# A convolution and gated two-layer network on one core: the first step's exchanges, loads and copies put in another order

## The chip, the cores and the metric

The kernel runs on one core of a Trainium2 chip. The metric is the device time of one execution in microseconds (us). A core has five engines that run their own instruction streams: TensorE (PE in the profile; its weight loads are PEld), VectorE (DVE), ScalarE (ACT), GpSimd (POOL) and SyncE (SP). SP, GpSimd and ScalarE also issue transfers (DMA), which sixteen DMA engines carry out. Results of matrix products come to lie in PSUM, eight banks of 128 x 512 words, here named `slot`; everything else is in SBUF, 128 partitions wide.

## The reference: what is computed

A causal depthwise convolution with seven taps, then two matrix products with a gate between them, in float32:

```python
w = exp(weight - max); w = w / (sum(w) + 1e-9)          # 8 heads x 7 taps
y[b, s, :] = sum_k w[head, k] * x_pad[b, s + k, :]      # x: 8 x 4096 x 192, 24 channels per head
h = y.reshape(32768, 192) @ w_in                        # w_in: 192 x 2048
g = h * (1 / (1 + exp(-1.702 * h)))
out = g @ w_out                                         # w_out: 2048 x 192
```

`x` and the taps come as float32; `w_in` and `w_out` come as 64-bit floating point, so the kernel itself takes their words apart and rounds them to 32 bits.

## The kernel before, in words

**Tiling and steps.** The tokens are worked through in 32 steps, which the code numbers by `big`; each has 1024 tokens, 512 consecutive ones of two sequences, the first 256 of each in one half of the partitions and the other 256 in the other half. A step transposes its x to channels on partitions (`transpose_x`, VectorE, L143), convolves it (`conv`, seven multiply-adds on VectorE, L162 and L164) into `own`, multiplies by `w_in` (the first product), applies the gate on ScalarE (`gelu`, L235) into the big buffer `g`, multiplies `g` by `w_out` (the second product, L513), transposes back and stores. From the second step on the first product runs at L212 as three passes: x and the weights are split into a high part, a low part and a difference (`xh`, `xl`, `xd` of x, `wh`, `wl` and stage tiles of the weights). The high parts `wh` and half of the low parts stay in SBUF, while the other parts stream from a scratch in DRAM, `w_dram`, through seven places of `ring` (`load_ring`, L199).

**Step 0** (`first_step`, with `second_plain` for its second product) does the same work while the weights themselves are still being loaded and prepared. `w_in` comes in four parts (`raw`, L321), each with 256 columns in one half of the partitions and the next 256 in the other. Each goes through `take` (exponent and mantissa, VectorE, L371 and L372), `clamp` (two ACTIVATEs on ScalarE, L377 and L378), `join` (L386 and L389) and `rounded` (L397). `split` is `take` and `clamp` together. From a rounded part, `top` makes `wh` (ScalarE, L425), `rest` the remainder (VectorE, L428), `spread` the low part (ScalarE, L435) and `differ` the difference (VectorE, L439). `put` stores a part's pieces to `w_dram` (L449). Then `w_out`, again in four parts (`raw_out`, L326), goes through the same rounding, in the order 1, 2, 3, 0.

Since a half of the partitions holds only half the columns of a part of `w_in`, each half of x must also meet the weights of the other half. So x is exchanged between the halves: `exchange` (L672) issues two SBUF-to-SBUF transfers on SP. `swapped[c]` are the exchanged copies of `own` in the place of `xt`; `swapped_h`, `swapped_l` and `swapped_d` those of `xh`, `xl` and `xd`, in places of `wh` and `wl` that are not in use yet. The first product of step 0 goes in sixteen groups: groups 0 to 3 with the first part of the weights in plain float32 (`plain`, L691), groups 4 to 15 in three passes (`quick`, L682), four groups a part: the first two on the core's own x, the next two on the exchanged x. A group takes up two banks of PSUM, and ScalarE's gelus of a group free them for the group four places on.

Behind the first product, `second_plain` starts (L513), and at its first row the rest of the preparation is issued: part 0's `top`, `rest`, `spread`, `differ` and `put`; `across`, which copies the finished halves of `wh` and `wl` to the other half of the partitions (L443); the split of step 1's x; the first loads of the ring; and the sums of the second product's weights (`FORMS_O`) on VectorE. Step 1's first product (`unit`, L212) follows on PE.

**What sets the order.** The order is written out by hand: each engine, and each engine's DMA queue, carries out its instructions in the order of the program, and an instruction waits for the semaphores of what it needs. So a transfer that waits on SP holds back every later transfer of SP, and a clamp on ScalarE stands behind the gelus that are written ahead of it. In `first_step` SP issues x's first batch, `w_in`'s first part, x's second batch and the other parts; then the exchanges of own for the three channel groups, xh, xl, the first part of `w_out`, and xd. GpSimd issues the stores of part 1 and the three other parts of `w_out`. SP follows with the stores of part 2, the x of step 1, the stores of part 3 and the x of step 2. Two of the three channel groups of step 0's convolution are done on PE with diagonal weights (`first_conv`, L657), the third on VectorE.

Of the kernel before, what the change touches and what calls it, by code (L numbers as in the profile page):

```python
# [16 lines left out]
def kernel(  # L17
# [9 lines left out]
    nc = tc.nc  # L27
# [10 lines left out]
    T = 256  # L38
# [32 lines left out]
    def wide(t):  # L71
        return t.bitcast(F32)
# [52 lines left out]
    def load_x(big, ns=(0, 1), os=(0, 1), queue=nc.sync):  # L125

        p, c = divmod(big, CHUNKS)
        xin = xin_of(big)
        if c == 0 and (ns[0], os[0]) == (0, 0):
            vec.memset(xin[0:R, :, 0, :], 0.0)  # L130
        for n in ns:
            for o in os:
                j = 1 if c == 0 and o == 0 else 0
                t = c * TOK + o * T + (j - 1) * Q
                for v in range(2):
                    q0 = o * R + v * Q
                    queue.dma_start(  # L137
                        out=xin[q0 : q0 + Q, n, j:NJ, :],
                        in_=x_v[n, p, t : t + (NJ - j) * Q, v * Q : v * Q + XW].rearrange("(j i) d -> i j d", i=Q),
                    )  # L140
# [13 lines left out]
    def own_of(c, of=own):  # L154
        return of[:, 2 * c : 2 * c + 2, :]
# [9 lines left out]
                out=dst, in0=src, scalar=tap, in1=dst, op0=ALU.mult, op1=ALU.add  # L165
            )

    def split_high(src=own):
        act.mul(xh, src, NEAR)

    def split_low(src=own):
        vec.scalar_tensor_tensor(out=xl, in0=src, scalar=UP, in1=wide(xh), op0=ALU.mult, op1=ALU.subtract)  # L172
# [146 lines left out]
    def load_w_in(i):  # L319
        for o in range(2):  # L320
            nc.sync.dma_start(  # L321
                out=raw[i][halves[o], :].bitcast(U32).rearrange("p (k f) -> p k f", k=NC), in_=w_in_v[2 * i + o]
            )

    def load_w_out(i, queue=nc.sync):
        queue.dma_start(  # L326
            out=raw_out[i].bitcast(U32).rearrange("p (c d) -> p c d", c=CW),
            in_=w_out_v[:, i * CW : (i + 1) * CW, :],
        )

    load_x(0, (0,))
    load_w_in(0)
    load_x(0, (1,))
    for i in range(1, N_IN):
        load_w_in(i)

# [43 lines left out]
    def split(piece):  # L380
        take(piece)
        clamp(piece)
# [55 lines left out]
        for r in range(2):  # L438
            vec.tensor_sub(stage(i)[:, 2 * r], wide(lows(i)[r]), half(wide(pair_of(i)), r))  # L439

    def across(t):
        for o, queue in enumerate((nc.sync, nc.gpsimd)):
            queue.dma_start(out=wide(t[halves[1 - o], N_IN:]), in_=wide(t[halves[o], :N_IN]))  # L443

    def put(i, queues=(nc.gpsimd, nc.gpsimd)):
        for o, queue in enumerate(queues):
# [251 lines left out]
    def first_step(tiles):  # L698

        for c in (1, 2):  # L700
            for k in range(K):
                act.mul(diag[:, c - 1, k, :], ident, cw[:, c, k : k + 1])
        for c in (1, 2, 0):
            transpose_x(0, c, 0, 1)
        first_conv(1, 0)
        first_conv(2, 0)
        for k in range(K):
            conv(0, k, n=0)
        split(part(0))
        for c in (1, 2, 0):  # L710
            transpose_x(0, c, 1, 2)
        first_conv(1, 1)
        act.copy(own_of(1), pairs[1][0].rearrange("p (n t) -> p n t", n=2))
        first_conv(2, 1)
        join(part(0))
        exchange(swapped[1], own_of(1))
        for k in range(K):
            conv(0, k, n=1)
        exchange(swapped[0], own_of(0))
        act.copy(own_of(2), pairs[1][1].rearrange("p (n t) -> p n t", n=2))  # L720
        exchange(swapped[2], own_of(2))
        rounded_in(0)
        early = osbs[:, 0 : 2 * NC * T].rearrange("p (b t) -> p b t", t=T)
        pieces = (1, 2, 3, 0)
        one, two, three, last = (part(N_IN + i) for i in pieces)
        split_high()
        exchange(wide(swapped_h), wide(xh))
        split(part(1))
        take(part(2))
        clamp(part(2))  # L730
        split_low()
        exchange(wide(swapped_l), wide(xl))
        load_w_out(pieces[0])
        round_w_in(1)

        def products(*groups):
            for i in groups:
                (quick if i >= 4 else plain)(tiles, i // 4, i // 2 % 2, i % 2)

        def gelus(*groups):  # L740
            for i in groups:
                r, s = 4 * (i // 4) + i % 2, i // 2 % 2
                for h in range(2):
                    gelu(tiles[(r + 2 * h) % 4], r + 2 * h, (h ^ s,))

        products(0, 1)
        gelus(0)
        top(1)
        gelus(1)
        split_both()  # L750
        exchange(wide(swapped_d), wide(xd))
        rest(1)
        spread(1)
        split(part(3))
        differ(1)
        put(1)
        for a in pieces[1:]:
            load_w_out(a, nc.gpsimd)
        round_w_in(2)
        products(2, 3)  # L760
        gelus(2, 3)
        top(2)
        products(4)
        gelus(4)
        join(part(3))
        rest(2)
        spread(2)
        rounded_in(3)
        top(3)
        differ(2)  # L770
        put(2, (nc.sync, nc.sync))
        load_x(1)
        products(5, 6)
        gelus(5, 6)
        rest(3)
        take(one)
        products(7)
        spread(3)
        gelus(7)
        clamp(one)  # L780
        differ(3)
        take(two)
        put(3, (nc.sync, nc.sync))
        round_w_out(pieces[0])
        products(8, 9)
        gelus(8, 9)
        clamp(two)
        take(three)
        round_w_out(pieces[1])
        products(10, 11)  # L790
        gelus(10, 11)
        clamp(three)
        products(12, 13)
        gelus(12, 13)
        take(last)
        round_w_out(pieces[2])
        products(14)
        gelus(14)
        clamp(last)
        products(15)  # L800
        gelus(15)
        round_w_out(pieces[3])
        for c in range(NC):
            transpose_x(1, c)
        for k in range(K):
            for c in range(NC):
                conv(c, k, early)

        pf, pa, pb, pc = tiles[3], tiles[1], tiles[0], tiles[2]
        load_x(2)  # L810

        def at(i):
            if i == 0:
                top(0)
                rest(0)
                spread(0)
                differ(0)
                put(0, (nc.sync, nc.gpsimd))
                across(wh)
                across(wl)  # L820
                split_high(early)
                split_low(early)
                split_both(early)
                for i in range(STREAM, STREAM + RING):
                    load_ring(i)
                for c in range(NC):
                    transpose_x(2, c)
                for item in FORMS_O:
                    add_form(*item)

        turns = second_plain(pb, pa, pc, at)
        unit(1, [pf], 0)
        for m, n, src in turns:
            turn(m, n, src, slice(0, TOK // Q))
            if m:
                store(0, n)
        return [pf, pa, pb, pc]
# [57 lines left out]
```

## Time and profile before

| | |
|---|---|
| median of 3 runs | 2179.86 us (2176.53 to 2179.95) |
| profiled execution | 2179.55 us, its span 2177.8 us |
| PE busy | 2165.8 us, 99% of the span |
| DVE, ACT, POOL busy | 1776.9, 986.6, 327.6 us |
| first plain product (L691) starts | 20.50 us |
| first quick product (L682) starts | 30.48 us |
| second product of step 0 (L513) starts | 62.94 us |
| step 1's first product (L212) starts | 104.28 us |

The profile gives, for one execution, the busy time of each engine, groups of instructions by line of the code, the chain of work that ended last (followed back from the end, at each step to what released it), the waits with their releasers, and the transfers with their sizes and their time from issue to landing. A row such as `slot<-xh,wh` names the tile written and the tiles read, without numbers of buffers. Times are counted from the start of the span. Busy time of PE is modelled with overlap, so a busy share of 99% does not say that PE runs at its peak; the granted clock is given beside it, where 1.00 is full. GB/s of the stretches is what the DMA engines moved, and a share somewhat above 1 in a stretch comes from packets that reach over its edges.

### The profile page before, as it was taken

To read this page: it belongs to the slowest core of one execution; us is meant where nothing else is said; L and a number is where in the kernel's file an instruction comes from. 1 tells how busy PE (TensorE), PEld (TensorE's weight loads), DVE (VectorE), ACT (ScalarE), POOL (GpSimd) and SP (SyncE) were. 2 spreads that over 40 slices of the span, in tenths; PEclk is the share of its full clock that TensorE was granted. 3 is DMA by queue.
4 is the path that set the end of the run, shared out by engine and by line. 5 is a ranking of instruction groups with operands and counts; after the bars stand their busy time and mean duration, and the time that the engine had idled before them with its cause. 6 is when DMAs were issued, how large, how long until landed. Compare 5 with 4: busy or idle time off the path is not lost.

```text
span 2177.8 us, 66287 instructions
## 1 busy us (share of the span) xinstructions
PE 2165.8 (99%) x28998; PEld 1521.4 (70%) x28998; DVE 1776.9 (82%) x2500; ACT 986.6 (45%) x2104; POOL 327.6 (15%) x444
## 2 busy tenths in 40 slices
PE   8999999999999999999999999999999999999999
PEld 7477766677766777667777667776677766677766
DVE  7888888888887878888888878788888888787766
ACT  6344444444444544444444445444444444444443
POOL 1101121011111111110111111111101111111000
PEclk9999999999999999999999999999999999999999
DMA  9666666575665666665756657565666666575554
GB/s 268 170 161 165 161 144 146 138 179 147 165 147 130 172 157 161 147 144 143 177 151 157 150 129 179 151 165 145 139 152 172 156 152 150 126 186 147 137 119 99
DMA packets 264707, 336.66 MB, mean 155 GB/s; under 512 B 121169, under 2 KB 226577, under 8 KB 264289
## 3 DMA queue, kind: packets, MB, share of 16 engines
q0 software_dynamic: 42848, 145.37, 31.8%
q1 hardware_dynamic: 219920, 186.66, 30.4%
q8 instruction: 227, 3.72, 0.7%
q10 hardware_dynamic: 1648, 0.39, 0.1%
q14 instruction: 64, 0.52, 0.1%
HBM read 199.43 MB, written 29.88 MB: 105 GB/s over the span
## 4 chain that ended last, share of the span: by engine, by line
PE 97%; DMA 1%; DVE 1%; SPq 0%; issue 0%; DVEq 0%
PE slot L513 50%; PE slot L212 46%; PE slot L682 1%; DMA wl<-xd 1%; DMA ring<-w_dram 0%; DMA g<-in_x_dram 0%; SPq L137 0%; DVE own L164 0%; DVE osbs L500 0%; DVE w_form L389 0%; DVE xl L172 0%; DVE w_form L386 0%; DVE xd L175 0%; DVE w_form L397 0%; SPq L510 0%
## 5 line engine op out<-in xcount | busy, mean ns | idle before, releaser
L513 PE MATMUL slot<-g,w_form 128*32 128x256 f32 x8928 | 894.1, 379 | 0.0
L235 ACT ACTIVATE g<-slot 128x512 f32<-128x512 f32 x1024 | 556.2, 596 | 506.7 <-PE slot L212 501.2
L576 DVE TENSOR_TENSOR g<-g 128x1024 f32<-128x1024 f32 x403 | 483.7, 1219 | 213.2 <-ACT g L235 124.5
L513 PEld LDWEIGHTS slot<-g,w_form 128*32 128x32 f32 x8928 | 480.6, 110 | 138.1
L624 ACT COPY room<-slot 32x256 f32<-32x256 f32 x651 | 238.3, 366 | 627.4 <-PE slot L513 625.3
L513 PE MATMUL slot<-g,w_out_s 128*32 128x256 f32 (+1 forms) x6336 | 508.8, 392 | 0.0
L212 PE MATMUL slot<-xh,wh 64*128 64x512 f32 x2976 | 422.6, 389 | 0.0
L212 PE MATMUL slot<-xd,ring 64*128 64x512 f32 x2976 | 418.6, 387 | 0.2 <-DMA ring<-w_dram 0.2
L513 PEld LDWEIGHTS slot<-g,w_out_s 128*32 128x32 f32 x6336 | 254.0, 110 | 204.1 <-issue 38.7
L164 DVE SCALAR_TENSOR_TENSOR own<-xt,cw,own 128x512 f32<-128x512 f32 (+1 forms) x552 | 365.7, 731 | 0.4
L212 PEld LDWEIGHTS slot<-xh,wh 64*128 64x128 f32 x2976 | 276.7, 184 | 69.8 <-issue 13.2
L212 PEld LDWEIGHTS slot<-xd,ring 64*128 64x128 f32 x2976 | 278.9, 184 | 59.1 <-DMA ring<-w_dram 0.6
L581 POOL DMA_DIRECT2D g<-g x124 | 117.1, 944 | 759.4 <-PE slot L513 520.8
L513 PE MATMUL slot<-osbs,w_form 128*32 128x256 f32 x2232 | 225.3, 379 | 0.0
L137 POOL DMA_DIRECT2D g<-in_x_dram x232 | 155.3, 676 | 401.1 <-PE slot L513 397.4
L212 PE MATMUL slot<-xl,wl 64*128 64x512 f32 x1488 | 209.4, 387 | 0.0
L212 PE MATMUL slot<-xl,ring 64*128 64x512 f32 x1488 | 209.1, 386 | 0.0
L513 PE MATMUL slot<-room,w_form 128*32 128x256 f32 x2232 | 171.6, 379 | 0.0
L212 PEld LDWEIGHTS slot<-xl,wl 64*128 64x128 f32 x1488 | 139.5, 184 | 30.0
L212 PEld LDWEIGHTS slot<-xl,ring 64*128 64x128 f32 x1488 | 139.5, 184 | 29.3
L513 PEld LDWEIGHTS slot<-osbs,w_form 128*32 128x32 f32 x2232 | 117.5, 110 | 42.5
L576 DVE TENSOR_TENSOR room<-slot,room 96x256 f32<-96x256 f32 x248 | 100.1, 414 | 57.1 <-PE slot L513 55.0
(114 smaller groups left out, 1379.0 us busy)
## 6 DMA issues: line engine op xcount, KB each, us to landing
ring<-w_dram SPq DMA_DIRECT2D x744, 192.0 KB, 2.7
g<-g POOLq DMA_DIRECT2D x124, 512.0 KB, 6.6
g<-in_x_dram POOLq DMA_DIRECT2D x220, 180.0 KB, 4.7
out_dram<-osbs SPq DMA_DIRECT2D x186, 128.0 KB, 5.5
g<-osbs POOLq DMA_DIRECT2D x31, 512.0 KB, 5.6
g<-room POOLq DMA_DIRECT2D x31, 512.0 KB, 6.6
g<-in_moe_w_in_dram SPq DMA_DIRECT2D x8, 384.0 KB, 9.5
w_dram<-ring SPq DMA_DIRECT2D x10, 288.0 KB, 5.0
```

Of the source, the lines that this page charges most:

```text
L137: queue.dma_start(out=xin[q0 : q0 + Q, n, j:NJ, :], in_=x_v[n, p, t : t + (NJ - j) * Q, v * Q : v * Q + XW].rearrange("(j i) d -> i j d", ...
L164: vec.scalar_tensor_tensor(out=dst, in0=src, scalar=tap, in1=dst, op0=ALU.mult, op1=ALU.add)
L212: nc.tensor.matmul(slot[o], w(o)[halves[o], k, :], t[halves[o], 2 * k : 2 * k + 2, :], start=first and k == KS[0], stop=last and k == KS[- ...
L235: act.activation(g[:, r // NG, :, o, r % NG, :], slot[o].rearrange("p (n t) -> p n t", n=2), AF.Gelu_apprx_sigmoid,)
L513: nc.tensor.matmul(dst, w, t, start=first, stop=last, skip_group_check=True)
L576: (eng.tensor_add if op == "+" else eng.tensor_sub)(v(dst), v(a), v(b))
L581: nc.gpsimd.dma_start(out=spot(dst), in_=spot(a), accum_op=ALU.add)
L624: act.copy(to, d)
L682: nc.tensor.matmul(tiles[2 * h + r][h ^ s], w[halves[h], c, :], xs[s][halves[h], 2 * c : 2 * c + 2, :], start=n == 0 and c == KS[0], stop= ...
```

## The change

Only step 0 is touched, in five places.

- x's second batch is issued on SP ahead of the first part of `w_in`. On VectorE, the transposes of that batch and four of the seven taps of its convolution move ahead of the first part's `take`; its `join` follows behind the last three taps. On SP the exchange of own's second channel group is issued before the convolution's last taps in program order.
- The exchange of xh is dropped. ScalarE makes `swapped_h` from the exchanged own instead, with a second `split_high`, behind `spread(1)`; `split_high` gets a destination for it.
- The first part of `w_out` (piece 1) is loaded behind the exchange of xd and behind `differ(1)` in program order, no longer ahead of it.
- The stores of part 1 and the other three loads of `w_out` are issued by SP instead of GpSimd; `load_w_out` loses its queue argument.
- `across` takes a range of parts. Parts 1 to 3 are copied behind the last quick product and step 1's convolution, ahead of the load of step 2's x; part 0 in the old place.

```diff
-    def split_high(src=own):
-        act.mul(xh, src, NEAR)
+    def split_high(src=own, dst=xh):
+        act.mul(dst, src, NEAR)
...
-    def load_w_out(i, queue=nc.sync):
-        queue.dma_start(
+    def load_w_out(i):
+        nc.sync.dma_start(
...
     load_x(0, (0,))
+    load_x(0, (1,))
     load_w_in(0)
-    load_x(0, (1,))
...
-    def across(t):
+    def across(t, i0, i1):
         for o, queue in enumerate((nc.sync, nc.gpsimd)):
-            queue.dma_start(out=wide(t[halves[1 - o], N_IN:]), in_=wide(t[halves[o], :N_IN]))
+            queue.dma_start(out=wide(t[halves[1 - o], N_IN + i0 : N_IN + i1]), in_=wide(t[halves[o], i0:i1]))
...
         for k in range(K):
             conv(0, k, n=0)
-        split(part(0))
         for c in (1, 2, 0):
             transpose_x(0, c, 1, 2)
+        for k in range(4):
+            conv(0, k, n=1)
+        split(part(0))
         first_conv(1, 1)
         act.copy(own_of(1), pairs[1][0].rearrange("p (n t) -> p n t", n=2))
         first_conv(2, 1)
+        exchange(swapped[1], own_of(1))
+        for k in range(4, K):
+            conv(0, k, n=1)
         join(part(0))
-        exchange(swapped[1], own_of(1))
-        for k in range(K):
-            conv(0, k, n=1)
         exchange(swapped[0], own_of(0))
...
         split_high()
-        exchange(wide(swapped_h), wide(xh))
         split(part(1))
...
         exchange(wide(swapped_l), wide(xl))
-        load_w_out(pieces[0])
         round_w_in(1)
...
         spread(1)
+        split_high(xt[:, :, :, 0:T].rearrange("p c n t -> p (c n) t"), swapped_h)
         split(part(3))
         differ(1)
-        put(1)
+        load_w_out(pieces[0])
+        put(1, (nc.sync, nc.sync))
         for a in pieces[1:]:
-            load_w_out(a, nc.gpsimd)
+            load_w_out(a)
...
         pf, pa, pb, pc = tiles[3], tiles[1], tiles[0], tiles[2]
+        across(wh, 1, N_IN)
+        across(wl, 1, N_IN)
         load_x(2)
...
                 put(0, (nc.sync, nc.gpsimd))
-                across(wh)
-                across(wl)
+                across(wh, 0, 1)
+                across(wl, 0, 1)
```

## The prediction, as it was put on record

> **What bounds the kernel now.** I read the page's head first, then the chain of waits in order of time, then stretches of the span, then the transfers. The head tells little by itself:
>
> ```profile
> span 2177.8 us, 66287 instructions
> ```
>
> The span stands beside 2179.55 us for the same execution (1.75 us lie around it), and 2179.86 us is the median of the runs shown, 0.31 above; the sum is made against 2179.55. The chain, with start, length and what ended last:
>
> ```profile
> 5.78 7.22 DMA g<-in_x_dram
> ...
> 28.90 12.10 DMA wl<-xd
> ...
> 41.05 21.96 PE slot L682 x164
> 63.01 41.34 PE slot L513 x384
> 104.35 5.66 PE slot L212 x47
> ```
>
> TensorE (PE) sets the end from 41.05 on without a break, so step 0 is worth what the moment is worth at which its second product (L513, 63.01) starts. Ahead of that stand two transfers: x's second batch (till 13.0) and the exchange of xd (till 41.0). The stretches show what the second costs (columns: PE, weight loads, VectorE = DVE, ScalarE = ACT, GpSimd, granted clock, DMA share, GB/s; the counts take in matmuls that overlap an edge):
>
> ```profile
> 36.80:39.00 2.20, 0.00 (x0) 0.00 (x0) 2.20 (x4) 2.20 (x5) 0.00 (x0) 1.00 0.96 311
> 39.00:41.00 2.00, 0.50 (x1) 0.18 (x1) 1.12 (x3) 0.16 (x1) 0.00 (x0) 0.72 1.02 410
> 41.00:43.00 2.00, 1.95 (x10) 1.58 (x12) 0.00 (x0) 0.69 (x2) 0.00 (x0) 0.50 1.01 406
> 43.00:45.00 2.00, 2.00 (x12) 1.59 (x10) 0.56 (x1) 0.81 (x2) 0.00 (x0) 0.50 1.04 417
> 45.00:46.90 1.90, 1.90 (x12) 1.49 (x10) 0.26 (x1) 1.27 (x3) 0.00 (x0) 0.55 1.03 411
> ...
> 50.00:62.90 12.90, 12.90 (x115) 11.53 (x111) 9.60 (x16) 10.79 (x19) 0.00 (x0) 1.00 0.75 195
> sum 32.90, PE 29.14 PEld 25.08 DVE 23.54 ACT 24.97 POOL 5.00; mean PE 3.24 PEld 2.79 DVE 2.62 ACT 2.77 POOL 0.56
> ```
>
> PE stops at 36.80, runs one matmul at 39, and goes on at 41.05: 4.25 us less one matmul, 4.1 lost. Then the clock is granted at 0.50 to 0.55 until 46.9. At full clock a matmul comes every 12.90/115 = 0.112 us (0.113 with the edges); the chain's 164 would take 18.6 us and took 21.96: 3.4 lost. The stall is worth 7.5 us in all. The sum row covers 30.0 to 62.9 and will be needed for ACT.
>
> Next the transfers, each with its KB and its median time from issue to landing:
>
> ```profile
> g<-in_moe_w_in_dram SPq DMA_DIRECT2D x8, 384.0 KB, 9.5
> ...
> w_dram<-ring POOLq DMA_DIRECT2D x4, 288.0 KB, 9.1
> xt<-own SPq DMA_DIRECT2D x6, 128.0 KB, 6.1
> wh<-xh SPq DMA_DIRECT2D x2, 384.0 KB, 7.1
> wh<-xl SPq DMA_DIRECT2D x2, 384.0 KB, 9.3
> g<-in_moe_w_out_dram SPq DMA_DIRECT2D x1, 768.0 KB, 11.6
> wl<-xd SPq DMA_DIRECT2D x2, 384.0 KB, 11.4
> g<-in_moe_w_out_dram POOLq DMA_DIRECT2D x1, 768.0 KB, 11.3
> ...
> g<-in_x_dram SPq DMA_DIRECT2D x4, 180.0 KB, 5.2
> g<-in_x_dram SPq DMA_DIRECT2D x4, 160.0 KB, 2.8
> ```
>
> and the rate at which they move (last two columns):
>
> ```profile
> 15.00:20.00 5.00, 5.00 (x24) 4.08 (x22) 4.79 (x10) 0.58 (x1) 0.00 (x0) 1.00 1.07 226
> 20.00:25.00 5.00, 4.54 (x22) 4.03 (x23) 5.00 (x8) 4.82 (x6) 0.00 (x0) 1.00 1.12 251
> 25.00:30.00 5.00, 5.00 (x26) 3.90 (x24) 4.96 (x6) 4.28 (x8) 0.00 (x0) 1.00 1.04 231
> ```
>
> The transfers of SyncE (SP) up to xd come to 8.47 MB: x 1.39, w_in 3.15, own 0.79, and xh, xl, the first w_out and xd 0.79 each. Counted from about 1.5 us on at 0.23 MB a us they are through at 38, and each lands about 2 us behind its last byte (x's second batch closes 2.18 MB, through at 11.0, and landed at 13.0 by the chain). This count gives all arrivals below. So the 12.10 us of xd are a queue, not a long transfer: two transfers of its own size (xh, w_out) stand in it, and GpSimd's stores and w_out loads come in beside it.
>
> **The change, part by part.** *x's second batch ahead of w_in(0), and conv(0) around split(part(0)).* These rows tell what they touch (the bracket is the idle time before and its releaser):
>
> ```profile
> 13.20 1.20 DVE L143 STREAM_TRANSPOSE xt<-g 128x288 f32<-128x288 f32 x3 [1.71 <-DMA g<-in_x_dram]
> ...
> 13.73 6.31 PE L657 MATMUL slot<-xt,room 128*128 128x256 f32 x28 [0.98 <-DVE xt L143]
> ...
> 20.50 5.63 PE L691 MATMUL slot<-own,w_form 64*128 64x512 f32 x24 [0.46 <-DVE w_form L397]
> 20.70 1.48 ACT L169 ACTIVATE xh<-own 128x1536 fp32r<-128x1536 f32 x1
> ```
>
> VectorE waits 1.71 us for that batch, PE's convolutions 0.98 behind it, and the first product (L691) starts at 20.50, 0.46 after PE was free. In the new order the batch has only x ahead of it (1.39 MB): it lands at about 9.6, before VectorE is free. w_in(0) then closes the 2.18 MB that the batch closed before, so it lands near 13.0. VectorE, free at about 10.5 (13.20 less the wait, less the takes of part 0 that stood ahead), does the transposes (1.20) and four conv steps (about 1.9) and comes to its first take at 13.6: hidden by 0.6, and beyond that each us of lateness costs one. The clamp of part 0 runs on ScalarE beside conv steps 4 to 6. PE's convolutions follow one another without their 0.98 and end at 19.05 (before: 20.50 less 0.46); VectorE's chain, 1.71 shorter, has the rounded weights at 18.8 to 18.9; so L691 starts at about 19.1: gain 1.4. split_high (the row of L169), which needs the copy of convolution 2, comes 1.0 sooner (19.7), and VectorE's chain behind it, to xd, too: the second half of xd is issued at 27.9, not 28.90.
>
> *Reach of that gain.* PE now comes to the second half of x (24.3) while the exchanges of own, of unchanged bytes, land as before: they close 5.33 MB, through at 24.7, landed at 26.7; the last of them is needed two thirds into a product, 26.1. Cost 0 to 0.9; I take 0.4.
>
> *High part made by ScalarE.* It removes 0.79 MB and two issues on SP, and adds one ACTIVATE of the form shown, 1.48 us, behind spread(1). Its input has landed by then (26.7 against 29.1, when ScalarE comes to it). Behind it on ScalarE wait the clamp of part 3, the gelus of groups 2 and 3, top(2): they come 1.48 later, less the 1.0 gained. PE needs gelus(2) only two products on, which covers it. But ScalarE's reserve shrinks: 24.97 us busy between 30.0 and 62.9, now 26.45, against 216 matmuls at 0.113 = 24.5 on PE. At worst it ends 26.45 less 24.5, 2.0 us, behind PE; but the last clamp's two ACTIVATEs are not ahead of the second product, which brings it level. Cost 0 to 2.0; I take 0.5, nearer the low end, for the waits for top(2) and rest(2) between the engines.
>
> *First w_out, stores of step 1 and the other w_outs behind xd, all on SP.* xl and xd now have only own ahead: 6.9 MB are through at about 31.5, xd lands at 33 to 34. PE asks for it 16.3 us after L691's start (20.50 to 36.80), at 19.1 + 16.3 + 0.4 = 35.8. Hidden, with 2 us to spare: the 7.5 us go. Late next are the w_outs: 0.79 + 1.18 (four stores) + 2.36 MB behind 31.5. The rate on SP where a w_out passes alone:
>
> ```profile
> DMA packets 332, 0.65 MB, mean 327 GB/s; under 512 B 13, under 2 KB 297, under 8 KB 331
> ```
>
> (32.9 to 34.9.) At 0.327 for w_out and 0.23 for stores the second w_out lands at 43, the last at 48; counted along the order of ScalarE's and VectorE's work (an estimate), VectorE comes to the second at 41.3, though the clamp of it stands only at 45, and to the last at 51. SP's own issuing of seven transfers more delays put(2) and the load of x(1), which waits in the queue anyway; x(1) lands at 56 to 58 (put(2) and x(1), 2.6 MB at 0.23 behind 46, less what overlaps). VectorE comes to it now at
>
> ```profile
> 65.65 2.09 DVE L143 STREAM_TRANSPOSE xt<-room 128x576 f32<-128x576 f32 x3
> ```
>
> and 8 us sooner would be 57.6. Cost 0; without cover 0.7 (second rival). GpSimd's queue had nothing behind these but copies that wait for later work.
>
> *Copies in two goes.* Three quarters of 2.36 MB move from the start of the second product's stage, ahead of the first loads of the ring, to the time right after the last quick product, when the DMA engines are nearly idle (0.75 share and falling in the last stretch). VectorE's longest wait thereafter:
>
> ```profile
> DVE osbs L500 <- ACT room L530: 5.2, 1, 5.2
> ```
>
> By the chain PE goes from 63.01 through 104.35 without a wait for the ring, so 0 gained; the ring's loads come up to 1.77/0.25 = 7 us sooner, which covers a late x(1), as VectorE's 5.2 us do. On SP load_x(2) stands behind the early copies, but it waits for the transposes of x(1), which are later. Cost 0.
>
> **Sum:** −1.4 + 0.4 + 0.5 − 7.5 = −8.0, so 2179.55 − 8.0 = 2171.55.
>
> **The rivals.** *xd still late.* If SP's queue runs 10% slower, or landing takes longer, PE waits at 35.8 again. For it: all DMA engines are at 1.0 share, and the margin is 2 us. Against: nothing but SP's own transfers is then in flight. Two us of lateness cost 2.0, and with the clock falling as it did (0.72 within the wait, then 0.50) 3.4 more: 2173.5 to 2177. The Trainium skill, "TensorE: Matmul & The Clock Gate", What's actually happening, has the clock halve after at least one idle window of about 3.4 us: a wait of 2 would then cost 2.0 alone, 2173.5. The trace agrees in the halving and in a recovery that takes some us; its clock had fallen within a wait of 4.25 broken by one matmul, so it can't show the shorter case.
>
> *One queue is slower than two.* While SP alone ran, 226 to 251 GB/s (stretches 15 to 30); while GpSimd's ran beside it, 406 to 417. If the queue, not the shape of the transfers, is the cap, the w_outs come at 0.226: the third at 49, VectorE reads the second's words (in the part of g that gelus(12) overwrites) until 52.4, and the second product starts 0.7 to 2 late: 2172.3 to 2173.5. Against: the 327 above, on SP alone. By the Trainium skill, "DMA: Bandwidth & Descriptors", Issuing engines are not separate DMA queues, all issuers share the same engines and more issuers save only issue time; then this rival falls and 2171.55 stands. The two rates agree with it only if shape explains them.
>
> *The start is earned and given back.* DVE is 9.60 of 12.90 busy in the last stretch; if its chain of joins, or x(1), moves only 0 to 3 us forward where PE moves 8, the second product or the next step waits for the rest: 2176.5 to 2179.6. For it: VectorE's 23.54 us in the sum row leave little under 24.5 of matmuls. Against: it idled 3.3 us of the last stretch, and its joins wait for ScalarE's clamps, which move with PE.
>
> *Slower.* x(1) now stands behind 13.8 MB on one queue. VectorE's chain from it (transposes, conv, rest(0), the stores, the ring) gates PE at 104.35. It costs as soon as x(1) lands later than about 65.65 plus the 7 us that the copies free; to end above 2184, it has to land after 77, which needs 6.9 MB in 45 us, 153 GB/s, and no row of SP is so slow.
>
> **How the numbers follow.** Forecast 0.65, alone 2170.1 (own and ScalarE cost nothing) to 2173; xd late 0.15; one queue 0.07; given back 0.09; slower 0.04. What a measurement can tell from no change is about 0.2%, 4.4 us: faster ends at 2175.5. Forecast, one queue, and four fifths of xd late lie under it, 0.84, with a little of given back (a median 1 us low) 0.86; same 0.10; slower 0.04. The range takes in forecast, xd late and one queue with the run-to-run spread (2176.53 to 2179.95): 2169 to 2176.5.
>
> **What would show it.** L691 at 19 without VectorE's wait for x; one more L169 of 1.48 us and no wh<-xh; xd landing about 5 us after its issue; no wait of L682 for wl<-xd, clock 1.00 throughout 30 to 63; L513 from about 54.5 to 55; w_outs landing under 50. Wrong if PE waits at L682 for a DMA or for ScalarE in sum over 3 us, or if L212's start moves much less than L513's.

## The result, and the profile after

| | before | after |
|---|---|---|
| median of 7 runs | 2179.23 us (2176.53 to 2179.95) | 2171.65 us (2171.39 to 2172.79) |
| profiled execution | 2179.55 us, span 2177.8 | 2171.48 us, span 2169.8 |
| first plain product (L691) starts | 20.50 | 18.85 |
| first quick product (L682) starts | 30.48 | 29.67 |
| second product of step 0 (L513) starts | 62.94 | 55.23 |
| step 1's first product (L212) starts | 104.28 | 96.56 |

The changed kernel takes 0.9969 of the time of the kernel before, with a 95% interval of 0.9958 to 0.9981. The two profiled spans differ by 8.0 us, and 7.71 of them are there when the second product starts. What follows lasts as long as before to within 0.3 us.

The chain of waits of the changed kernel, in order of time (start, length, what ended last):

```profile
18.85 11.38 PE slot L691 x45
30.23 0.10 PE slot L682
30.34 0.35 PE slot L691
30.69 24.60 PE slot L682 x213
55.30 41.34 PE slot L513 x384
96.63 15.41 PE slot L212 x133
```

No transfer stands in it any more, neither x's second batch nor xd. The stretches in which PE stood and then ran at half clock now read (columns as in the prediction):

```profile
36.80:39.00 2.20, 2.20 (x23) 2.20 (x21) 2.20 (x5) 2.20 (x6) 0.00 (x0) 1.00 0.90 274
39.00:41.00 2.00, 2.00 (x20) 2.00 (x19) 1.54 (x4) 2.00 (x6) 0.00 (x0) 1.00 1.03 353
41.00:43.00 2.00, 2.00 (x21) 2.00 (x19) 1.06 (x4) 1.97 (x3) 0.00 (x0) 1.00 1.07 375
43.00:45.00 2.00, 2.00 (x21) 2.00 (x19) 1.97 (x3) 2.00 (x6) 0.00 (x0) 1.00 0.99 333
45.00:46.90 1.90, 1.90 (x21) 1.90 (x19) 1.87 (x5) 1.87 (x4) 0.00 (x0) 1.00 1.06 399
```

PE is busy throughout, at a clock of 1.00, with 20 matmuls or more in each of the two stretches that had none and one. Next the transfers of the first 60 us (KB each, median time from issue to landing), among them the exchange of xl, that of xd, and the w_outs on SP:

```profile
g<-in_moe_w_out_dram SPq DMA_DIRECT2D x2, 768.0 KB, 8.3
room<-in_x_dram SPq DMA_DIRECT2D x8, 180.0 KB, 5.9
xt<-own SPq DMA_DIRECT2D x6, 128.0 KB, 6.2
wh<-xl SPq DMA_DIRECT2D x2, 384.0 KB, 5.9
wl<-xd SPq DMA_DIRECT2D x2, 384.0 KB, 4.6
osbs<-in_moe_w_out_dram SPq DMA_DIRECT2D x1, 768.0 KB, 9.3
room<-in_moe_w_out_dram SPq DMA_DIRECT2D x1, 768.0 KB, 9.9
```

The exchange of xd is the same 384 KB twice and takes 4.6 us instead of 11.4: it was the queue. Three rows show the other edits (VectorE's transposes of x's second batch, the second high part on ScalarE, the store of part 1 on SP):

```profile
10.46 1.19 DVE L143 STREAM_TRANSPOSE xt<-g 128x288 f32<-128x288 f32 x3
...
28.90 1.47 ACT L169 ACTIVATE wh<-xt 128x1536 fp32r<-128x1536 f32 x1
...
29.92 5.07 SPq L449 DMA_DIRECT2D w_dram<-ring  x4
```

The 1.71 us of waiting ahead of the transposes are gone. One new wait is there, PE's (at the weight load) for the exchanges of own, in products 2 and 3:

```profile
PEld slot L691 <- DMA xt<-own: 1.0, 2, 0.8
```

### The profile page after: what moved, and what is told of

Read it like the earlier page. It is cut to its first block, busy times and chain, and to the rows that moved or that the text cites. A ratio compares the mean times of both kernels' runs of the same rounds, so it can differ in the third digit from the quotient of the medians.

```text
span 2169.8 us, 66285 instructions
## 1 busy us (share of the span) xinstructions
PE 2163.2 (100%) x28998; PEld 1519.6 (70%) x28998; DVE 1776.9 (82%) x2500; ACT 988.6 (46%) x2105; POOL 324.6 (15%) x439
## 4 chain that ended last, share of the span: by engine, by line
PE 100%; DVE 0%; POOL 0%; issue 0%; POOLq 0%
PE slot L513 50%; PE slot L212 47%; PE slot L682 1%; PE slot L657 1%; PE slot L691 1%; PE slot L474 0%; PE slot L478 0%; DVE osbs L500 0%; DVE room L576 0%; POOL osbs masks.py:199 0%; POOL osbs masks.py:197 0%; POOLq masks.py:199 0%; POOLq L883 0%
## 5 line engine op out<-in xcount | busy, mean ns | idle before, releaser
L513 PE MATMUL slot<-g,w_form 128*32 128x256 f32 x8928 | 894.1, 379 | 0.0
L513 PEld LDWEIGHTS slot<-g,w_form 128*32 128x32 f32 x8928 | 479.7, 110 | 138.4
L513 PE MATMUL slot<-g,w_out_s 128*32 128x256 f32 (+1 forms) x6336 | 508.7, 392 | 0.0
L212 PE MATMUL slot<-xh,wh 64*128 64x512 f32 x2976 | 422.4, 389 | 0.0
L212 PE MATMUL slot<-xd,ring 64*128 64x512 f32 x2976 | 418.4, 386 | 0.0
L513 PEld LDWEIGHTS slot<-g,w_out_s 128*32 128x32 f32 x6336 | 254.0, 110 | 204.5 <-issue 38.8
L212 PEld LDWEIGHTS slot<-xh,wh 64*128 64x128 f32 x2976 | 276.4, 184 | 70.0 <-issue 13.2
L212 PEld LDWEIGHTS slot<-xd,ring 64*128 64x128 f32 x2976 | 278.7, 184 | 58.8
L513 PE MATMUL slot<-osbs,w_form 128*32 128x256 f32 x2232 | 225.3, 379 | 0.0
L212 PE MATMUL slot<-xl,wl 64*128 64x512 f32 x1488 | 209.4, 386 | 0.0
L212 PE MATMUL slot<-xl,ring 64*128 64x512 f32 x1488 | 209.0, 386 | 0.0
L513 PE MATMUL slot<-room,w_form 128*32 128x256 f32 x2232 | 171.5, 379 | 0.0
L212 PEld LDWEIGHTS slot<-xl,wl 64*128 64x128 f32 x1488 | 139.4, 184 | 30.1
L212 PEld LDWEIGHTS slot<-xl,ring 64*128 64x128 f32 x1488 | 139.4, 184 | 29.4
L513 PEld LDWEIGHTS slot<-osbs,w_form 128*32 128x32 f32 x2232 | 117.4, 110 | 42.6
```

The lines of the kernel that those rows point to most:

```text
L212: nc.tensor.matmul(slot[o], w(o)[halves[o], k, :], t[halves[o], 2 * k : 2 * k + 2, :], start=first and k == KS[0], stop=last and k == KS[- ...
L513: nc.tensor.matmul(dst, w, t, start=first, stop=last, skip_group_check=True)
```

## The experiments

Two theories about the whole were set against each other. By the queue theory, PE runs on without a break once xd arrives before PE asks for it, and xd's arrival is set by the bytes ahead of it on SP; an edit is worth what it does to that meeting. By the sum theory, each edit brings its own share. The contention theory adds that GpSimd's transfers hold xd up from the side. The start of the second product (L513) is read from each profile; ratios are against the kernel before on the same chip.

**Front alone.** The kernel before, with this edit only:

```diff
     load_x(0, (0,))
+    load_x(0, (1,))
     load_w_in(0)
-    load_x(0, (1,))
...
-        split(part(0))
         for c in (1, 2, 0):
             transpose_x(0, c, 1, 2)
+        for k in range(4):
+            conv(0, k, n=1)
+        split(part(0))
...
+        exchange(swapped[1], own_of(1))
+        for k in range(4, K):
+            conv(0, k, n=1)
         join(part(0))
-        exchange(swapped[1], own_of(1))
-        for k in range(K):
-            conv(0, k, n=1)
```

> The kernel before with the front alone: x's second batch ahead of w_in(0), four conv steps ahead of split(part(0)), everything else as before. Queue theory (the arrival of xd is set by the bytes ahead of it on SP, and PE meets it there): the first product (L691) starts at 18.9 instead of 20.5, but 8.47 MB still stand up to xd, which lands at 40 to 41; PE only comes sooner to a wait that is longer by the same 1.6 us; the second product (L513) starts at 62.5 to 63.0, the time is 0 to 0.5 us lower. Sum theory (each edit brings its own gain): L513 at 61.5, time 1.2 to 1.6 us lower.

Measured: 2178.0 us, ratio 1.0 (0.999 to 1.0009); L691 starts at 18.98, L513 at 62.83. Its chain of waits:

```profile
28.54 12.97 DMA wl<-xd
41.51 0.04 issue
41.55 21.35 PE slot L682 x165
62.90 41.34 PE slot L513 x384
```

PE's first product comes 1.5 us sooner, and nothing of it is left at the second: the exchange of xd is issued a little sooner, and lands half a us later than before. The sum theory wanted 1.2 to 1.6 us. So a gain ahead of a transfer that is bound by its queue is worth nothing.

**No exchange of xh, alone.** The kernel before, with

```diff
-    def split_high(src=own):
-        act.mul(xh, src, NEAR)
+    def split_high(src=own, dst=xh):
+        act.mul(dst, src, NEAR)
...
         split_high()
-        exchange(wide(swapped_h), wide(xh))
...
         spread(1)
+        split_high(xt[:, :, :, 0:T].rearrange("p c n t -> p (c n) t"), swapped_h)
         split(part(3))
```

> The kernel before with the exchange of xh replaced by the second high part on ScalarE, nothing else. Queue theory: 7.68 MB up to xd, through at 34.9 and landed at about 37, PE wants it at 36.8: the wait shrinks from 4.25 to under 0.5 us, the clock stays at 1.00, L513 starts at 55.7 to 56.7, the time is 6.5 to 7.5 us lower. Sum theory (each 0.79 MB taken from ahead of xd brings its half of 7.5): L513 at 59.3, 3.5 to 4 us lower. Contention theory (GpSimd's stores and loads beside xd hold it up): xd lands at 38.5 to 39, wait of 2 with a lowered clock after it, L513 at 59 to 61, 2 to 4 us lower.

Measured: 2172.73 us, ratio 0.9976 (0.9967 to 0.9986), L513 at 56.93.

```profile
29.36 8.24 DMA wl<-xd
37.60 0.04 issue
37.65 19.35 PE slot L682 x167
57.00 41.34 PE slot L513 x384
```

xd lands at 37.6, PE waits 0.4 us for it (its weight load 0.9), and 167 matmuls take 19.35 us (0.116 each); the clock stayed at 1.00 from 35 to 45. One taking of 0.79 MB from ahead of xd brought 6.0 of the 7.7 us at L513, not half. GpSimd's stores and loads were beside xd in this run and did not hold it up by more than the 0.7 us by which it missed the count of 36.9; the contention theory wanted 38.5 to 39.

**First w_out, stores and w_outs behind xd on SP, alone.** The kernel before, with

```diff
         exchange(wide(swapped_l), wide(xl))
-        load_w_out(pieces[0])
         round_w_in(1)
...
         differ(1)
-        put(1)
+        load_w_out(pieces[0])
+        put(1, (nc.sync, nc.sync))
         for a in pieces[1:]:
-            load_w_out(a, nc.gpsimd)
+            load_w_out(a)
```

> The kernel before with the first w_out, the stores of part 1 and the other w_outs behind xd on SP, nothing else (the exchange of xh stays). Queue theory: the same 7.68 MB up to xd, landed at about 37, no GpSimd traffic beside it: wait under 0.5 us, L513 at 55.5 to 56.5, the time 6.5 to 7.5 us lower, so that this and the edit on xh are each nearly enough alone. Sum theory: 3.5 to 4 us lower. Contention theory: here xd is free, 7.5 us lower, while the run without the exchange of xh is not.

Measured: 2173.53 us, ratio 0.9978 (0.9969 to 0.9986), L513 at 56.28. Two rows of its waits, PE's for xd and, later, the one for the ring:

```profile
PE slot L682 <- DMA wl<-xd: 0.4, 1, 0.4
PEld slot L212 <- DMA ring<-w_dram: 0.5, 1, 0.5
```

Again nearly all of it from one edit. The second row is a first sign of what stands behind: with PE 6.7 us sooner and the copies still in one go, the ring came 0.5 us late.

**Both put back.** The changed kernel, with the exchange of xh and the first w_out ahead of xd again; front, stores, other w_outs and copies stay changed:

```diff
         split_high()
+        exchange(wide(swapped_h), wide(xh))
...
         exchange(wide(swapped_l), wide(xl))
+        load_w_out(pieces[0])
...
-        split_high(xt[:, :, :, 0:T].rearrange("p c n t -> p (c n) t"), swapped_h)
...
-        load_w_out(pieces[0])
```

> The changed kernel with the exchange of xh put back (no second high part on ScalarE) and the first w_out ahead of xd again; front, stores and other w_outs on SP, copies in two goes stay. Queue theory: 8.47 MB up to xd as before, no GpSimd traffic beside it: xd lands at 38.5 to 39.5, PE wants it at 35.5, wait 3 to 4 us and a lowered clock after it; L513 at 60.5 to 61.5 (55.3 in the changed kernel), time 5 to 6.5 us over the changed one. Sum theory: 7.5 us over it. If the clock needs a full idle window of 3.4 us to fall, a wait just under that leaves it at 1.00 and costs 3 to 3.5 us alone.

Measured: 2177.66 us, ratio 0.9998 (0.9989 to 1.0007), L513 at 60.10. PE's rows and the stretches around the wait:

```profile
38.67 0.64 PE L682 MATMUL slot<-wl,ring 64*128 64x512 f32 x1 [2.38 <-DMA wl<-xd]
39.59 1.65 PE L682 MATMUL slot<-wl,ring 64*128 64x512 f32 x5 [0.29 <-DMA wl<-xd]
```
```profile
37.00:39.00 2.00, 0.33 (x1) 0.18 (x1) 2.00 (x4) 1.23 (x3) 0.00 (x0) 0.97 0.99 326
39.00:41.00 2.00, 1.71 (x7) 1.16 (x8) 0.19 (x1) 0.14 (x1) 0.00 (x0) 0.50 1.06 398
41.00:43.00 2.00, 2.00 (x14) 1.55 (x12) 0.28 (x1) 1.35 (x3) 0.00 (x0) 0.68 1.07 402
```

With 8.47 MB up to xd the stall is back, 3.3 us of it with the clock at 0.50 behind. The two takings are one thing: with either of them alone, in the two runs above, the wait was under a us, and without both it is whole. xd landed 1.5 us sooner than before the change (39.55 against 41.01), with no GpSimd traffic beside it: at most that much was contention, and the queue is the rest.

**Copies in one go.** The changed kernel, with

```diff
-        across(wh, 1, N_IN)
-        across(wl, 1, N_IN)
         load_x(2)
...
-                across(wh, 0, 1)
-                across(wl, 0, 1)
+                across(wh, 0, N_IN)
+                across(wl, 0, N_IN)
```

> The changed kernel with the copies across in one go at the old place. Copies-cost-nothing theory: VectorE's differ(0) still frees the stores of part 0 22 to 23 us ahead of PE's first use of the ring, as before the change, where PE did not wait; L513 at 55.3, L212 at 96.6, no PE wait for the ring beyond 0.5 us, time within 1 us of the changed kernel's. Rival (the copies in two goes are what keeps the ring in time once PE comes 8 us sooner): the first loads of the ring land up to 7 us later, PE waits 1 to 5 us at L212, time higher by as much.

Measured: 2172.02 us, ratio 0.997 (0.9958 to 0.9981), L513 at 55.41, L212 at 96.75.

```profile
PEld slot L212 <- DMA ring<-w_dram: 0.5, 1, 0.5
```

The ring comes 0.5 us late to a weight load. The chain of this run has that load landing at 108.6, inside step 1's first product, so the start of that product, 41.34 us after the second product's as in the changed kernel, does not show it. A cost of 0.5 us is less than these times can tell. The copies in two goes only restore a margin that was used up.

**Stores and the last three w_outs on GpSimd again.** The changed kernel, with `put(1)` and `load_w_out(a, nc.gpsimd)` as before:

```diff
-    def load_w_out(i):
-        nc.sync.dma_start(
+    def load_w_out(i, queue=nc.sync):
+        queue.dma_start(
...
-        put(1, (nc.sync, nc.sync))
+        put(1)
         for a in pieces[1:]:
-            load_w_out(a)
+            load_w_out(a, nc.gpsimd)
```

> The changed kernel with the stores of part 1 and the last three w_outs issued by GpSimd again (the first w_out stays on SP behind xd). Queue theory: these come behind xd's issue on either queue, and xd keeps at least 1.5 us of margin: no wait at L682, L513 at 55.0 to 55.6, time within 1 us of the changed kernel's. Contention theory: they run beside xd and hold it up by 1 to 2.5 us: PE waits up to 1 us at 35.5, L513 at 55.5 to 56.5.

Measured: 2171.76 us, ratio 0.9968 (0.9956 to 0.9981), no wait of L682. L513 started at 56.09, but the 0.8 us were there already at L682 (30.48 against 29.67), where these transfers had not begun: the first product of this execution began 0.4 us later (19.25), and it waited longer for own (1.5 us). From L682 to L513 it took 25.61 us, 25.56 in the changed kernel. So the issuing engine makes no difference here that could be seen, for xd or for the w_outs.

**Old front.** The changed kernel with the front of the kernel before, which is the first diff reversed:

```diff
     load_x(0, (0,))
-    load_x(0, (1,))
     load_w_in(0)
+    load_x(0, (1,))
...
+        split(part(0))
         for c in (1, 2, 0):
             transpose_x(0, c, 1, 2)
-        for k in range(4):
-            conv(0, k, n=1)
-        split(part(0))
...
+        join(part(0))
         exchange(swapped[1], own_of(1))
-        for k in range(4, K):
+        for k in range(K):
             conv(0, k, n=1)
-        join(part(0))
```

> The changed kernel with the old front (x's second batch behind w_in(0), conv behind the split of part 0). Now PE runs without a break from the first product to the second, so the front counts in full: L691 at 20.5 (18.85), L513 at 56.5 to 57.0 (55.3), time 1.2 to 1.7 us over the changed kernel's, while the same edit alone on the kernel before brought nothing. Rival (ScalarE's chain, not PE's, carries the stage): it moves by the 1.0 of split_high, L513 at 56.3, 1.0 us.

Measured: 2172.02 us, ratio 0.997 (0.9958 to 0.9981). Both theories named there miss:

```profile
20.05 5.63 PE L691 MATMUL slot<-own,w_form 64*128 64x512 f32 x24 [0.46 <-DVE w_form L397]
...
55.28 9.22 PE L513 MATMUL slot<-g,w_out_s 128*32 128x512 f32 x84
```

The first product starts 1.2 us later than in the changed kernel, the second 0.05. L691 to L682 takes 9.98 us here and 10.82 there: the wait for own, which the new front runs into, eats 0.84. The last 0.31 go between L682 and L513 (25.25 against 25.56): some 0.2 of it where the last plain matmuls overlap the first quick ones (the plain ones end at 30.84 here and at 30.69 there), the rest with no wait that the profile names. The front is worth nothing measurable in either kernel.

**Second high part made twice.** The changed kernel with one more ACTIVATE of 1.47 us:

```diff
         split_high(xt[:, :, :, 0:T].rearrange("p c n t -> p (c n) t"), swapped_h)
+        split_high(xt[:, :, :, 0:T].rearrange("p c n t -> p (c n) t"), swapped_h)
```

> The changed kernel with the second high part made twice on ScalarE (1.47 us more, no use). It measures ScalarE's reserve. If ScalarE is level with PE, as the prediction counted: L513 later by 0.7 to 1.5 us, PE waiting for gelus in groups 8 to 14. If ScalarE has a reserve of over 1.5 us: L513 within 0.3 us, no wait of L682 for a gelu.

Measured: 2172.12 us, ratio 0.9972 (0.9961 to 0.9983), L513 at 55.80.

```profile
PEld slot L682 <- ACT g L235: 0.5, 2, 0.3
```

From L682 to L513 takes 26.07 us, 0.51 more, and PE now waits for gelus. Of 1.47 us some 1.0 are hidden: that was ScalarE's reserve, and it is used up with one such instruction more.

**Exchange of xh back, alone.** The changed kernel, with

```diff
         split_high()
+        exchange(wide(swapped_h), wide(xh))
...
-        split_high(xt[:, :, :, 0:T].rearrange("p c n t -> p (c n) t"), swapped_h)
```

> The changed kernel with the exchange of xh put back and no second high part on ScalarE. Queue theory: 7.68 MB up to xd, which landed at 32.3 in the changed kernel and now lands 3.4 us later, 35.7, against PE's need at 35.5: wait 0 to 0.9 us, clock 1.00, L513 at 55.2 to 56.2, time within 1 us of the changed kernel's: of the two takings from ahead of xd one is enough. Sum theory: 3.5 us over the changed kernel.

Measured: 2173.66 us, ratio 0.9981 (0.9972 to 0.999), L513 at 56.27.

```profile
28.16 8.80 DMA wl<-xd
PEld slot L682 <- DMA wl<-xd: 1.4, 1, 1.4
```

xd lands at 37.0, and the queue theory misses twice: it had put the landing at 35.7 and the time within 1 us. It had only added 3.4 us to the landing in the changed kernel; the prediction's count of bytes gives 36.9 (7.68 MB at 0.23 MB a us from 1.5 on, and 2 us). From L682 to L513 takes 26.91 us, 1.35 more than in the changed kernel, which is the wait. L513 itself is 1.0 us later. The time is 2.0 us higher; the other 1.0 of this execution lies in later steps, where three weight loads of L212 waited 1.1 us for the ring. Whether the edit has to do with that stays open.

**First w_out ahead of xd, alone.** The changed kernel, with

```diff
         exchange(wide(swapped_l), wide(xl))
+        load_w_out(pieces[0])
...
-        load_w_out(pieces[0])
```

> The changed kernel with the first w_out ahead of xd again, the exchange of xh still replaced by ScalarE. Queue theory: as the run with the exchange of xh back, and sooner by up to 1 us, since w_out moved at 327 GB/s against 230: xd at 34.7 to 35.7, wait 0 to 0.5 us, L513 at 55.2 to 56.0, time within 1 us of the changed kernel's. Sum theory: 3.5 us over it.

Measured: 2172.04 us, ratio 0.9971 (0.996 to 0.9982), L513 at 55.39, no wait of L682. The same KB stand ahead of xd in these two. With xh they make xd land at 37.0, with w_out by 36.1, and there PE doesn't wait at all. A stretch of each, first with xh, then with w_out:

```profile
33.00:35.00 2.00, 2.00 (x22) 2.00 (x19) 2.00 (x4) 1.95 (x4) 0.00 (x0) 1.00 0.98 213
```
```profile
30.00:32.00 2.00, 2.00 (x18) 1.82 (x16) 1.97 (x3) 1.97 (x3) 0.00 (x0) 1.00 1.13 289
```

So w_out moved faster than the exchange. The edit on xh is worth 0.9 us more at L513 than the place of w_out (56.27 against 55.39), and 1.6 us of time on the same chip; w_out's place is worth nothing that can be seen, once xh is gone.

**A wait in between.** The changed kernel with the exchange of xh back and half of the first w_out ahead of xd:

```diff
-    def load_w_out(i):
+    def load_w_out(i, c0=0, c1=CW):
...
+        exchange(wide(swapped_h), wide(xh))
...
         exchange(wide(swapped_l), wide(xl))
+        load_w_out(pieces[0], 0, CW // 2)
...
-        split_high(xt[:, :, :, 0:T].rearrange("p c n t -> p (c n) t"), swapped_h)
...
-        load_w_out(pieces[0])
+        load_w_out(pieces[0], CW // 2)
```

> The changed kernel with the exchange of xh back and half of the first w_out (0.39 MB) ahead of xd, the other half behind: it makes a wait of 1.2 to 2.2 us at 35.5, between the waits seen so far. If the granted clock falls with any wait of that length: stretches behind it at 0.5 to 0.8 for some us, L513 at 57.5 to 59.5. If it needs a full idle window of 3.4 us: clock 1.00 throughout, L513 later by the wait alone, 56.5 to 57.5.

Measured: 2176.83 us, ratio 0.9991 (0.9982 to 1.0). In the profiled execution (2174.84 us):

```profile
37.46 0.49 PE L682 MATMUL slot<-wl,ring 64*128 64x512 f32 x1 [1.23 <-DMA wl<-xd]
38.97 0.96 PE L682 MATMUL slot<-wl,ring 64*128 64x512 f32 x5 [1.01 <-DMA wl<-xd]
```
```profile
37.00:39.00 2.00, 0.53 (x3) 0.22 (x3) 1.35 (x2) 1.34 (x3) 0.00 (x0) 1.00 1.05 352
39.00:41.00 2.00, 2.00 (x18) 1.65 (x20) 1.03 (x2) 1.26 (x3) 0.00 (x0) 1.00 1.06 398
41.00:43.00 2.00, 2.00 (x22) 1.65 (x20) 0.27 (x1) 0.24 (x1) 0.00 (x0) 1.00 1.07 400
```

PE stops for 2.7 us with one matmul in between, longer than the 1.2 to 2.2 that were meant, and the clock stays at 1.00. L513 starts at 58.23, 3.0 late, which is the wait and a little more. So there the clock did not fall with the wait. But the eleven runs fall into two groups: three of 2174.53 to 2174.84, the profiled one among them, and eight of 2176.59 to 2177.56. They lie 2.3 us apart, between the costs of a fallen clock in two other kernels: 1.5 with both put back (165 matmuls in 20.58 us against 19.1 at the pace of 167 in 19.35) and 3.0 in the kernel before (164 in 21.96 against 19.0). That the eight are those in which the clock fell is an inference; none of them was profiled.

**w_in's last part behind own.** The changed kernel, with

```diff
-    for i in range(1, N_IN):
+    for i in range(1, N_IN - 1):
         load_w_in(i)
...
         exchange(swapped[2], own_of(2))
+        load_w_in(N_IN - 1)
```

> The changed kernel with the last part of w_in loaded behind the exchanges of own instead of ahead of them. Theory: what the front gained (L691 at 18.85) is eaten in products 2 and 3, which wait for own's exchanges behind all of w_in in the queue (L691 to L682 took 10.82 us, 9.98 before the change). Now own lands 3.4 us sooner, the wait goes, L682 starts at 28.8 to 29.0 (29.67), L513 at 54.3 to 54.7 (55.3), time 0.6 to 1 us lower. The last part lands at 26.7, VectorE takes it at 27.9. Rival (ScalarE or VectorE, not own, holds the stage): L682 sooner, L513 unchanged at 55.2.

Measured: 2171.84 us, ratio 0.997 (0.9959 to 0.9982). L682 starts at 29.10, as expected, and PE does not wait for own any more. But L513 stays at 55.24:

```profile
28.06 7.87 DMA wl<-xd
35.93 0.04 issue
35.98 19.34 PE slot L682 x167
```

xd lands at least 3 us later than in the changed kernel (35.93 against 32.9 at the latest), though no more bytes stand ahead of it. The stretches ahead of it say why:

```profile
18.00:20.00 2.00, 2.00 (x9) 1.14 (x9) 2.00 (x4) 0.76 (x2) 0.00 (x0) 1.00 0.85 190
20.00:22.00 2.00, 2.00 (x11) 1.45 (x12) 1.29 (x3) 2.00 (x2) 0.00 (x0) 1.00 0.75 173
22.00:24.00 2.00, 2.00 (x12) 1.39 (x10) 2.00 (x3) 1.94 (x4) 0.00 (x0) 1.00 0.48 90
```

The queue ran empty (0.48 share, 90 GB/s, where the changed kernel has 263): w_in's last part had been what filled it while own was computed, and now it came late and took its time ahead of xl and xd. The gain at own was paid back at xd: from L682 to L513 takes 0.58 us more than in the changed kernel, of which 0.5 are a wait for xd at a weight load. The rival's figure came, but the wait that caused it is xd's and not ScalarE's or VectorE's. No version tried beats the changed kernel by more than these measurements can tell.

## Why the prediction was right, step by step

**The whole.** It put the time of its execution at 2171.55; the profiled one took 2171.48, and the median is 2171.65. The mechanism, xd's place in its queue, is what the runs show. That the sum agrees to 0.1 us is partly luck in the terms, as follows.

**The stall: right.** It counted −7.5 for the stall and +0.5 for ScalarE between the quick products' start and the second product; that stretch went from 32.46 us to 25.56, −6.9 against −7.0. xd was issued at 27.2 and 27.7 and landed within 5.2, so by 32.9, where 33 to 34 was counted. Two of its terms were too large and made up for each other: the fallen clock was priced at 3.4, from 0.113 us a matmul, where the pace behind a wait at full clock (167 matmuls in 19.35 us) makes it 3.0, and ScalarE's 0.5 is taken up below. The count of bytes at 0.23 MB a us, with 2 us for landing, which the prediction took from x's second batch alone, met the arrivals of xd to within 2 us in the runs on the kernel before and the changed one; it is 2.4 us off where the queue runs empty, as in the last run (33.5 counted, 35.93). The prediction did not see that one of the two takings would nearly do. It took the 7.5 us as the work of all together, and its margin of 2 us (3 in the trace) could have told it: 0.79 MB more are 3.4 us, so 1.4 us of waiting, which is what the run with the exchange of xh back shows.

**The front: the step that failed.** "Reach of that gain" took 0.4 for own, out of a range of 0 to 0.9, against a gain of 1.4, so net −1.0. L691 did start at 18.85 (19.1 was counted), but the wait for own cost 0.84, and the run with the old front shows that net nothing is left. The mechanism was named, and its size was near the upper end: own's arrival is bound by the bytes of w_in ahead of it, as xd's was (with w_in's last part behind own the wait is gone), and a chain that comes 1.65 us sooner meets it 1.65 us sooner. The missing 1.0 us did not show in the time by luck. The run with the old front started its first product at 20.05, 0.45 sooner than the kernel before with the same front, and took 25.25 us from L682 to L513, 7.2 less than before where 7.0 were counted. The other 0.3 came behind L513, where nothing was counted.

**ScalarE: right in kind, too dear.** It was counted as level with PE, at a cost of 0.5. The doubled high part shows that about 1.0 us more could be hidden beside the instruction that the change adds, and the changed kernel has no wait of PE for a gelu in the quick products.

**w_outs and x(1): hidden, as counted.** The w_out issued last, at 37.35, landed within 10 us, under 50, and VectorE took up x(1) without waiting for it at 57.92, against 57.6 in the prediction. The rival that one queue is slower than two finds no support: with the transfers on GpSimd again the stage took the same 25.6 us, and the changed kernel, whose SP alone carries everything, moved 333 to 399 GB/s from 39 to 47. By the Trainium skill, "DMA: Bandwidth & Descriptors", Issuing engines are not separate DMA queues, transfers run on the same 16 DMA engines whichever engine issued them. The trace agrees: 25.61 us with GpSimd issuing, 25.56 with SP.

**Copies: cost nothing, as counted,** and gained at most the 0.5 us by which the ring is late without them.

**The rival "xd still late"** did not come to pass, but the runs that brought it about by hand price it. Waits of 0.9 and 1.4 us at the weight load (no exchange of xh alone; xh back) cost no more than themselves up to L513. A stop of 3.3 us with one matmul in it (both put back) brought the clock to 0.50 and cost 1.5 us beyond the wait; one of 2.7 us left the clock at 1.00 in the execution that was profiled. The front alone has the clock falling with no matmul in the gap (the stretch, and PE's row behind the gap):

```profile
39.00:41.00 2.00, 0.79 (x1) 0.29 (x1) 0.35 (x1) 0.00 (x0) 0.00 (x0) 0.51 1.02 369
```
```profile
39.96 0.79 PE L682 MATMUL slot<-wl,ring 64*128 64x512 f32 x1 [3.26 <-DMA wl<-xd]
```

A mean of 0.51 from 39 on means that it fell at about 39.05, 2.3 us after PE's last matmul had ended (39.96 less 3.26, so 36.70). With both put back the mean of 0.97 from 37 to 39 puts the fall at 38.9, 2.6 us after the last matmul ahead of the stop (38.67 less 2.38, so 36.29). The Trainium skill, "TensorE: Matmul & The Clock Gate", What's actually happening, says that the clock halves after at least one idle window of about 3.4 us, and that the window runs freely. The traces agree that waits of up to 1.4 us leave the clock alone, but they do not bear out that length: the clock fell 2.3 and 2.6 us into a stop, and the measurement decides. Since it fell 2.3 us into one stop and had not fallen after 2.7 us in another, the runs do not settle which of the prediction's two prices holds for a wait of 2 us; the 3.4 us on top are more than the 1.5 measured with both put back. Nothing here shows where a window began. The rivals "given back" and "slower" found nothing to stand on.

## What to carry to other kernels

Where a chain of waits runs through a transfer, count the bytes ahead of it in its queue first: here that count told its landing to within 2 us as long as the queue never ran empty, and it told what a gain ahead of it is worth, which can be nothing. Edits that take bytes from ahead of the same transfer did not add up here; either one alone took most of the gain, so try each alone before keeping all of them. And when the order of a queue is changed, look for the moment at which it runs empty: a load that stands in the way there may be what fills the gap.

## What had not been expected of the hardware

Equal KB were not equal time. Exchanges between the halves of the partitions, 64 partitions each, moved at 213 GB/s with the DMA engines at a share of 0.98 (33 to 35, in the run with xh back), while the load of w_out into all 128 partitions moved at 327 on the same queue before the change; ahead of xd that made 0.9 us or more (landed at 37.0 with xh, by 36.1 with w_out). The parts of w_in, which come from DRAM into 64 partitions each, moved at 226 GB/s (15 to 20 before the change), so the low rate seems to go with the half of the partitions and not with the source. No run changes the number of partitions alone.

The spread from run to run is larger with the stall, though not strictly. The kernel before, on the chip of the first four runs, spread over 6.5 us (2174.04 to 2180.57, 32 runs), both put back over 5.0 and the wait in between over 3.0 (11 runs each). The kernels with no wait for xd of more than 0.5 us spread over 0.9 to 1.9 us (5 to 7 runs each; ScalarE's doubled instruction, with its short waits for gelus, 2.6). But more runs reach further apart by themselves, and two runs don't fit: the front alone, with the whole stall, and the first w_out behind xd, with a wait of under a us, both spread over 3.0 (11 runs each). The two groups of the run with the wait in between suggest a reason, a clock that falls in some runs and not in others, but no profile here shows a run of each kind.
